# K chunks of a cached-attention decode kernel: in-place transposes in three parts instead of two

## The chip, the cores and the metric

The kernel runs on one core of a Trainium2 chip. Five engines of that core work from their own instruction queues: TensorE (PE, with its weight loads shown as PEld), VectorE (DVE), ScalarE (ACT), GpSimd (POOL) and SyncE (SP). SP does no arithmetic here; it issues nearly all the transfers from the chip's memory (HBM) into the core's working memory. The engines wait for each other through semaphores. The metric is the device time of one execution in microseconds (us), lower is better. A time is given as the median of several executions.

## The reference, cut to what matters

```python
def _A_ref(x, k_cache, v_cache, wq, wo):          # x [8,1,448]; caches [8, 8, 4096, 256]
    q = (x @ wq) -> [8, 16 heads, 1, 256]
    k = repeat(k_cache, 2, axis=1); v = repeat(v_cache, 2, axis=1)
    scores = einsum("bhqd,bhkd->bhqk", q, k) * 256 ** -0.5
    p = softmax(scores)
    o = einsum("bhqk,bhkd->bhqd", p, v)
    return o.reshape(8, 1, 4096) @ wo
x = A_x
x = x + _A_ref(layernorm(x), ...)                 # pass 0
x = x + _B_ref(layernorm(x), w1, w2, w3, w4)      # an MLP
x = x + _A_ref(layernorm(x), ...)                 # pass 1, the same caches again
x = x + _B_ref(layernorm(x), w1, w2, w3, w4)
```

Everything is bf16. There are 8 batch elements with one token each, 16 query heads and 8 key/value heads, 4096 cached positions and a head dimension of 256. K and V are 134 MB each, and both passes read the same two caches. The arithmetic per byte is small: each cached value is used for two query heads and then no more in that pass. (`_B_ref` also has a branch on shifted columns; with one token per sequence every shift brings in zeros alone, so the kernel computes only the MLP of `w3` and `w4`.)

## The kernel before

**Tiling.** The key/value heads are taken in four pairs, called `gp`. One task is one pass, one batch element and one `gp`. Its K, two heads of 4096 positions of 256 values, comes as four chunks of 1 MB; so does its V. A chunk lies in one of `NC = 15` slots of 8 KB in each of 128 partitions (line 72), as 16 positions of 256 values in each partition.

**What stays.** 11 of the chunks of a batch element are kept in their slots from pass 0 until pass 1 of that element (`kept`, line 63), and a twelfth is parked in PSUM (`away` and `back`, lines 723 and 730). While they are kept, only the few slots left over carry the stream of all other chunks. Slots in plenty and slots in short supply alternate, once for each batch element.

**The order of work.** It is written out by hand. `items` (line 538) is a list of chunks: K chunks of a task, interleaved one to one with the V chunks of the task before it. The loop at line 834 goes through it and emits for a K chunk: `transpose_k` (line 870), one piece of the small work that is spread between the chunks (`step`, line 871), then `scores` and, after every second chunk, the exponentials `exps`. For a V chunk it emits one piece of small work and then `pv`, 16 matmuls. After either, the chunk's slot goes back to the list `places`, `emit_loads` (line 945) issues the next transfer into a slot that is free in this order, and another piece of small work follows. Each engine executes its share in exactly that order. SP waits, for every transfer, until the last user of the slot is done: for a K slot this is the last matmul of `scores`, for a V slot the last matmul of `pv`.

**The small work.** The generators `first_half`, `chain`, `first_last`, `last` and `rest` (lines 456 to 504) hold the normalization of the softmax, the output projection, the MLP and the next query projection of a batch element. They are chains of short DVE, ACT and POOL instructions and groups of matmuls with 128x128 weights; each piece needs the one before.

**The K chunk.** The scores need the head dimension on the partitions. `transpose_k` transposes the chunk in place with DVE, in blocks of 32 by 32 words of 32 bits (two bf16 values each). A partition's row of a chunk is 16 positions (`y`) of 128 words; the 128 words are four quarters (`e`) of 32 words. The loop of line 689 takes two instructions, one for quarters 0 and 1 of all positions and one for quarters 2 and 3. `scores` (line 693) then runs eight rounds `n`, each with four matmuls (`k`) that write to four different groups of 32 PSUM partitions: rounds 0 to 3 read quarters 0 and 1, rounds 4 and 5 read quarter 2, rounds 6 and 7 read quarter 3. Some chunks are taken in twos (`also`), when they lie in neighbouring slots. In round 4, `between` may put the transpose of the previous task's probabilities ahead of the second half.

A matmul waits for the DVE instruction that wrote what it reads, so the first half's matmuls can run while the second half is transposed.

Of the kernel before, what the change touches and what calls it, by code (L numbers as in the profile page):

```python
# [10 lines left out]
U32 = mybir.dt.uint32  # L11
# [6 lines left out]
def kernel(  # L18
# [530 lines left out]
    def stays(it):  # L549
        n, kv, c = it  # L550
        return (tasks[n][2], kv, c) in kept

    def inside(it):
        n, kv, c = it
        return (tasks[n][2], kv, c) == inner
# [130 lines left out]
    def transpose_k(t):  # L686


        for half in range(2):
            w = t[:].bitcast(U32).rearrange("p (y e w) -> p y e w", e=2, w=64)[:, :, half]  # L690
            nc.vector.transpose(w, w)  # L691

    def scores(t, x, qbd, gp, also=None, between=None):
# [140 lines left out]
    for idx, it in enumerate(items):  # L834
# [12 lines left out]
        p = where[(b, gp), (kv, c)] if ps == 1 and (stays(it) or inside(it)) else where[it]  # L847
# [3 lines left out]
        if kv == 0:  # L851
# [17 lines left out]
            if not (ps == 1 and stays(it)):  # L869
                transpose_k(slot)  # L870
# [142 lines left out]
```

## Time and profile before

| | |
|---|---|
| median of 4 executions | 1114.28 us (1108.36 to 1118.52) |
| the profiled execution, whole | 1118.52 us |
| its span, first to last instruction | 1116.7 us |
| memory read in it | 446.77 MB |
| PE busy | 664.1 us (59%) |
| ACT busy / POOL busy | 124.5 us (11%) / 16.4 us (1%) |
| transfers of V, 1 MB each | 215, median 13.1 us from issue to landing |
| transfers of K, 1 MB each | 154, median 8.8 us from issue to landing |
| transfers of K, 2 MB each | 23, median 17.5 us |

A transfer's time from issue to landing includes its queueing behind the transfers issued before it, so a short one means few were ahead of it. The busy share of an engine is an average over stages with different limits; PE's is also modelled, since matmuls overlap. DVE's work is nearly all in one group: the 400 transposes of line 691, two for each of 200 K chunks. In the chain of work that ended last, the largest parts are waits for K and V transfers.

The last 13 us of the span have no cache transfer: they are the last output projection, the MLP of four batch elements and the store of the result, after the last V chunk has landed.

### The profile page before, as it was taken

The page shows a single profiled execution, that of the slowest core. Times are in us where ns is not written, and L with a number is a line of the kernel's source. Part 1 is how long each engine was busy: PE and PEld are TensorE (multiplying, and loading weights), DVE is VectorE, ACT ScalarE, POOL GpSimd, SP SyncE. Part 2 cuts the span into 40 slices and gives each one's busy share as a digit, 9 for nine tenths or more (in the row PEclk, how much of TensorE's full clock was granted, in tenths as well). Part 3 has the DMA queues.
Part 4 walks back from the last instruction along what each step waited for, and adds up shares of the span by engine and source line. Part 5 has one row for each costly group of instructions (what it writes and reads, how often), then busy time and mean ns, then how long its engine had stood idle before and what let it go on. Part 6 is the DMA issues. An engine that isn't in the chain of part 4 may idle for free. (4 is left out here: it accounts for less than half of the span.)

```text
span 1116.7 us, 33251 instructions
## 1 busy us (share of the span) xinstructions
PE 664.1 (59%) x15350; PEld 457.0 (41%) x15350; DVE 590.8 (53%) x1010; ACT 124.5 (11%) x362; POOL 16.4 (1%) x27
## 2 busy tenths in 40 slices
PE   3235567556754577536684466744676467847775
PEld 2123445334532354324452244523454345635554
DVE  4245554646355555546365563665637552665372
ACT  0001001100110011101011000200111001111010
POOL 0000000000000000000000000000000000000000
PEclk9999999655565557655555555765556555565565
DMA  9999999999999999999999999999999999999994
GB/s 347 386 426 419 418 382 416 419 411 394 418 423 421 391 407 421 424 419 388 397 417 421 421 384 413 416 423 417 391 421 420 410 389 402 420 417 364 404 419 188
DMA packets 62012, 448.92 MB, mean 402 GB/s; under 512 B 6569, under 2 KB 10545, under 8 KB 11313
## 3 DMA queue, kind: packets, MB, share of 16 engines
q1 hardware_dynamic: 61680, 446.42, 97.9%
q8 instruction: 120, 1.97, 0.7%
q10 hardware_dynamic: 192, 0.38, 0.2%
q14 instruction: 20, 0.16, 0.0%
HBM read 446.77 MB, written 0.01 MB: 400 GB/s over the span
## 5 line engine op out<-in xcount | busy, mean ns | idle before, releaser
L691 DVE STREAM_TRANSPOSE places<-places 128x1024 uint32<-128x1024 uint32 x400 | 468.4, 1218 | 282.5 <-DMA places<-in_A_k_cache_dram 277.4
L706 PE MATMUL sc<-places,qbd 128*8 128x128 bf16 (+1 forms) x6816 | 269.1, 311 | 252.9 <-DVE places L691 206.7
L761 PE MATMUL o<-places,ptw 128*8 128x256 bf16 x3968 | 244.3, 390 | 143.3 <-DMA places<-in_A_v_cache_dram 130.6
L706 PEld LDWEIGHTS <-qbd 128*8 128x8 bf16 x6816 | 165.4, 106 | 332.8 <-issue 160.7
L761 PEld LDWEIGHTS <-ptw 128*8 128x8 bf16 x3968 | 114.3, 111 | 190.2 <-issue 149.2
L715 ACT ACTIVATE p_n<-sc 128x256 bf16<-128x256 f32 x128 | 95.7, 748 | 835.2 <-PE sc L706 835.2
L316 DVE TENSOR_SCALAR qbd<-misc,quad 128x64 bf16<-128x64 f32 x64 | 13.8, 277 | 64.1 <-PE misc L310 64.1
L343 PEld LDWEIGHTS <-wo_sb 128*128 128x128 bf16 x1280 | 38.4, 102 | 20.9 <-issue 20.8
L290 PEld LDWEIGHTS <-wq_sb 128*128 128x128 bf16 x1152 | 35.8, 104 | 26.4 <-issue 18.0
L290 PE MATMUL misc<-xb,wq_sb 128*128 128x1 bf16 x1024 | 34.4, 165 | 4.7 <-ACT ptw L749 3.2
L343 PE MATMUL misc<-OT,wo_sb 128*128 128x1 bf16 x1024 | 34.8, 165 | 3.5 <-issue 3.5
L715 ACT ACTIVATION_READ_ACCUMULATOR p_n<-sc 128x1 f32 x128 | 33.8, 264 | 0.0
L749 ACT CAST ptw<-misc 128x128 bf16<-128x128 f32 x64 | 17.5, 274 | 123.5 <-PE misc L742 64.5
L447 PEld LDWEIGHTS misc<-R,o_sb 128*128 128x128 f32 x124 | 26.2, 293 | 9.7 <-issue 8.1
L240 POOL TENSOR_TENSOR t<-t,nhalf 128x2 f32<-128x2 f32 (+2 forms) x20 | 14.0, 704 | 1087.3 <-DVE t L254 1087.3
L447 PE MATMUL misc<-R,o_sb 128*128 128x8 f32 x124 | 28.9, 343 | 0.3 <-ACT o_sb L442 0.3
L416 PE MATMUL misc<-zm,one 128*128 128x8 f32 (+1 forms) x66 | 19.2, 364 | 13.0 <-DVE zm L408 11.3
L733 DVE STREAM_TRANSPOSE places<-store 128x512 uint32<-128x512 uint32 x32 | 20.1, 684 | 12.3 <-PE sc L706 12.3
L416 PEld LDWEIGHTS misc<-zm,one 128*128 128x128 f32 x66 | 16.3, 307 | 19.6 <-issue 12.4
L361 PEld LDWEIGHTS <-w_sb 128*128 128x128 bf16 x560 | 17.3, 105 | 10.5 <-issue 10.4
L361 PE MATMUL misc<-xb,w_sb 128*128 128x1 bf16 (+1 forms) x560 | 18.6, 166 | 4.4 <-DVE xb L267 2.2
L726 DVE STREAM_TRANSPOSE store<-places 128x512 uint32<-128x512 uint32 x32 | 20.0, 693 | 1.5 <-DMA places<-in_A_v_cache_dram 1.4
(93 smaller groups left out, 227.8 us busy)
## 6 DMA issues: line engine op xcount, KB each, us to landing
places<-in_A_v_cache_dram SPq DMA_DIRECT2D x215, 1024.0 KB, 13.1
places<-in_A_k_cache_dram SPq DMA_DIRECT2D x154, 1024.0 KB, 8.8
places<-in_A_k_cache_dram SPq DMA_DIRECT2D x23, 2048.0 KB, 17.5
wo_sb<-in_A_wo_dram SPq DMA_DIRECT2D x1, 3584.0 KB, 27.5
wq_sb<-in_A_wq_dram SPq DMA_DIRECT2D x3, 1024.0 KB, 10.2
w_sb<-in_B_w_dram SPq DMA_DIRECT2D x1, 1568.0 KB
w_sb<-in_B_w_dram SPq DMA_DIRECT2D x3, 448.0 KB, 19.0
places<-in_A_v_cache_dram SPq DMA_DIRECT2D x2, 512.0 KB, 19.2
```

What stands on the lines that cost most here:

```text
L290: nc.tensor.matmul(q_ps[:, j * Hq + h, :], w, xbs(nb)[:, xi, :], start=(fc == 0), stop=(fc == 3),)
L343: nc.tensor.matmul(y_ps[:, fc, :], w[:, i, at : at + 128], rhs(i), start=start, stop=stop, skip_group_check=open is not None,)
L361: nc.tensor.matmul(h_ps[:, c * nb : c * nb + nb], w, xbs(nb)[:, xi, :], start=(fc == 0), stop=(fc == 3),)
L416: nc.tensor.matmul(z_ps, ones, zm[:], start=True, stop=True)
L447: nc.tensor.matmul(ot_ps[:, j], o_sb[:].rearrange("p (i j) -> p j i", j=2)[:, j], R[:], start=True, stop=True)
L691: nc.vector.transpose(w, w)
L706: nc.tensor.matmul(sc[32 * k : 32 * k + 8, 128 * x : 128 * (x + nx)], qbd[:, ep, gp].rearrange("p a h -> p (a h)"), v, start=(n == 0), sto ...
L715: nc.scalar.activation(p_sb[:, :, :, 2 * u : 2 * u + 2].rearrange("p t i x -> p x t i"), sc[:, 256 * u : 256 * u + 256].rearrange("p (x t ...
L726: nc.vector.transpose(store[n][:].bitcast(U32), slot[:].bitcast(U32)[:, 512 * n : 512 * n + 512])
L733: nc.vector.transpose(slot[:].bitcast(U32)[:, 512 * n : 512 * n + 512], store[n][:].bitcast(U32))
L749: nc.scalar.copy(ptw[:, :, :, 6:8], pt_ps.rearrange("p t k (a h) -> p a (t k) h", a=4),)
L761: nc.tensor.matmul(o_ps[32 * q : 32 * q + 8, 0:256], ptz[:, at : at + 8], v[:, y * Dh : (y + 1) * Dh], start=(begin and y < 4), stop=(y >= ...
```

## The change

`transpose_k` issues three instructions for each chunk instead of two: quarters 0 and 1 in one, then quarter 2, then quarter 3. The first is the same as before (16 runs of 64 words in each partition); the other two have 16 runs of 32 words.

```diff
     def transpose_k(t):
 
 
-        for half in range(2):
-            w = t[:].bitcast(U32).rearrange("p (y e w) -> p y e w", e=2, w=64)[:, :, half]
+        for e0, e1 in ((0, 2), (2, 3), (3, 4)):
+            w = t[:].bitcast(U32).rearrange("p (y e w) -> p y e w", e=4, w=32)[:, :, e0:e1]
             nc.vector.transpose(w, w)
```

`scores` has no change in its text. In the built program PE, ACT, POOL and SP have the same instructions in the same order as before. DVE has one more transpose for each K chunk. On PE one more matmul of each chunk waits for DVE: round 4 now waits for quarter 2 alone, and round 6 for quarter 3.

## The prediction

> **What bounds the kernel now.** I read the page first, for the engines and the transfers.
>
> ```profile
> span 1116.7 us, 33251 instructions
> DMA  9999999999999999999999999999999999999994
> GB/s 347 386 426 419 418 382 416 419 411 394 418 423 421 391 407 421 424 419 388 397 417 421 421 384 413 416 423 417 391 421 420 410 389 402 420 417 364 404 419 188
> q1 hardware_dynamic: 61680, 446.42, 97.9%
> ```
>
> The transfer queue that SP fills is busy 97.9% of the span, in every slice but the last. No engine comes near: DVE has 590.8 us, 53%. The kernel is bound by reading the caches. But the GB/s row shows more than the 9s: it runs at 416 to 426 and dips to between 364 and 397 at regular intervals, one dip for each batch element. A busy queue can still be a thin one. So the second view is the table of stages, with borders laid around two of the dips.
>
> ```profile
> core 0: us, PE busy (x) PEld busy (x) DVE busy (x) ACT busy (x) POOL busy (x), PEclk, DMA share, GB/s
> 570.00:640.00 70.00, 39.03 (x870) 25.53 (x866) 42.50 (x44) 7.89 (x22) 0.00 (x0) 0.55 1.01 422
> 640.00:700.00 60.00, 40.63 (x918) 28.39 (x912) 29.68 (x72) 6.48 (x22) 1.25 (x2) 0.50 0.99 399
> 820.00:890.00 70.00, 40.19 (x961) 27.00 (x960) 40.68 (x56) 9.63 (x28) 0.00 (x0) 0.60 1.01 421
> 890.00:950.00 60.00, 41.71 (x980) 29.83 (x984) 26.94 (x61) 6.48 (x19) 1.25 (x2) 0.50 0.98 392
> ```
>
> The reader is to see that DVE is busier in the stages that run at full rate (42.50 of 70 us) than in those that dip (29.68 of 60). DVE's load as such costs nothing. Full rate is about 421. All eight dips (130 to 180, 240 to 300, 370 to 430, 500 to 570, 640 to 700, 770 to 820, 890 to 950, 1000 to 1060 us, at 393, 403, 400, 397, 399, 401, 392 and 385) lose, against 421, 60 x (1 - 399/421) = 3.1 us in the fourth of those I show and so on: 3.3 + 2.6 + 3.0 + 4.0 + 3.1 + 2.4 + 4.1 + 5.1 = about 28 us together. That is all that a faster or slower handling of slots can act on from inside the stream; the start (first 50 us) and the 13 us after the last transfer have no K transposes on their path to speak of.
>
> The third view is the timeline inside a dip, which shows why it dips (lines in between left out).
>
> ```profile
> 649.36 0.33 SPq L678 DMA_DIRECT2D places<-in_A_k_cache_dram  x1
> ...
> 654.30 0.16 DVE L216 TENSOR_REDUCE t<-t 128x2 f32<-128x8 f32 x1
> ...
> 654.51 0.50 PEld L221 LDWEIGHTS misc<-t,one 128*128 128x128 f32 x2 [0.53 <-DVE t L216]
> ...
> 655.03 1.03 PE L761 MATMUL o<-places,ptw 128*8 128x256 bf16 x16
> ...
> 656.10 0.33 SPq L678 DMA_DIRECT2D places<-in_A_v_cache_dram  x1
> 656.70 2.37 DVE L691 STREAM_TRANSPOSE places<-places 128x1024 uint32<-128x1024 uint32 x2 [0.83 <-DMA places<-in_A_k_cache_dram]
> ...
> 658.00 0.60 PE L706 MATMUL sc<-places,qbd 128*8 128x128 bf16 x16 [1.94 <-DVE places L691]
> ...
> 659.13 0.60 PE L706 MATMUL sc<-places,qbd 128*8 128x128 bf16 x16 [0.53 <-DVE places L691]
> ...
> 659.77 0.33 SPq L678 DMA_DIRECT2D places<-in_A_k_cache_dram  x1
> ```
>
> This is one round of one K slot. Its transfer is issued at 649.36, has landed at 656.70 when DVE starts at once, the second half's matmuls end at 659.73, and SP issues into the slot at 659.77. Round: 10.41 us, of which 7.34 in flight and 3.07 on the core. A V slot works alike: the matmuls of L761 end at 656.06, SP issues at 656.10. Two K and two V slots carry the stream here, 4 MB a round; at 421 GB/s that is 9.96 us. So the round is 0.45 us longer than the transfers alone need, and each tenth taken off the core's 3.07 us can come back, until 0.45 is used up.
>
> **The change, part by part.**
>
> *DVE's extra instruction.* The nearest rows for a transpose of 512 words in a partition:
>
> ```profile
> L691 DVE STREAM_TRANSPOSE places<-places 128x1024 uint32<-128x1024 uint32 x400 | 468.4, 1218 | 282.5 <-DMA places<-in_A_k_cache_dram 277.4
> L726 DVE STREAM_TRANSPOSE store<-places 128x512 uint32<-128x512 uint32 x32 | 20.0, 693 | 1.5 <-DMA places<-in_A_v_cache_dram 1.4
> ```
>
> ```profile
> 94.22 2.50 DVE L726 STREAM_TRANSPOSE store<-places 128x512 uint32<-128x512 uint32 x4
> ...
> 186.62 9.12 DVE L691 STREAM_TRANSPOSE places<-places 128x1024 uint32<-128x1024 uint32 x8
> ```
>
> By whole durations, two of 512 cost 2 x 693 - 1218 = 168 ns more than one of 1024. But the merged rows show that transposes in a row overlap: four of 512 take 2.50 us, so a pitch of (2.50 - 0.69)/3 = 0.60; eight of 1024 take 9.12, a pitch of (9.12 - 1.20)/7 = 1.13. By pitch the cost is 2 x 0.60 - 1.13 = 0.07 us. The Trainium skill (VectorE: DVE Perf Modes, "The DRAIN you can't avoid") speaks against the change here: the next operation does not start until the pipe is empty, and one is told to minimize the number of operations. By that rule 168 ns a chunk, 200 x 0.168 = 34 us of DVE; by the trace 200 x 0.07 = 14 us. I take the trace, and keep 0.17 as the upper end. Lower end zero: L726 writes PSUM, and a write to the same memory may be no dearer. Shorter runs (32 words instead of 64) number 16 in either shape; 1024 in 16 runs has the pitch of 1.13 and 512 in one run 0.60, both the words at one per about 1.04 ns with 0.06 over, so the breaks between runs cost nothing that I can see.
>
> Where does this lie? In the full stages beside a stream that does not wait for it: the cover is 27.5 of 70 us idle on DVE. In the dips it lies in the path of every chunk.
>
> *The release of a K slot.* Before: transposes 2.37, then 0.06 to the first matmul of the second half, then 0.60. After: first part unchanged, 1.17 to its successor's start, then 0.60, then the last part 0.69: 2.46, so +0.09. Behind it come 8 matmuls instead of 16. One takes 0.31 (mean of the L706 row), four run side by side, so the 16 are four groups: (0.60 - 0.31)/3 = 0.10 a group, and two groups fewer save 0.19. Quarter 2's eight are done by then (ready at 1.17 + 0.69 = 1.86, done about 2.3). Net -0.10 us in a K release. Ends: -0.19 if a quarter costs no overhead, about 0 if parts do not overlap. PE's additional wait per chunk blocks what stands behind it (the small work, then L761), which PE reaches 0.10 earlier for the same reason; PE idles 0.53 us between the halves now, so it had nothing else there.
>
> *The release of a V slot.* The pieces of small work on DVE stand behind the transposes and go +0.07 later (ends 0 and +0.17). Where PE needs them before L761, as L221 at 654.51 waits for L216, the V slot comes free 0.07 later. Where it does not, 0.10 earlier. The rows of SP's waits name both kinds of release about equally often in this stage, so I count V as even.
>
> *The sum.* The stage from 640 to 700 has 16 transposes, 8 chunks: four rounds of two K slots. Four rounds x 0.10 = 0.4 us, eight dips: 3.2 us at most by this share. V rounds stand still, and a part of every dip is a late start rather than a tight round, so I take somewhat over half: -2 us. Against the profiled execution's own 1118.52 (span 1116.7 and 1.8 around it): 1116.5. This execution was the slowest of the four shown, 4.2 above the median of 1114.28, so the forecast is 1112.
>
> Whether there is anything to recover rests on the rate that the stream could have. The Trainium skill (DMA: Bandwidth & Descriptors, "Where 436 GB/s comes from") says that for transfers from HBM the memory's limit of about 358 GB/s for a core binds. By that rule the dips, at 385 and more, would be above the limit and nothing could be won or lost by slots. The trace has 70 us at 422; the measurement decides, and the dips are a shortage of slots.
>
> **The rivals.**
>
> *Nothing moves* (0.27). The stream is bound by bytes, and what the K slots gain the V slots lose. For: the queue's 97.9%, and 28 us as the whole of what slots can act on. Time: 1114.
>
> *Slower through the V slots* (0.18). Mechanism: in the dips a DVE piece behind the transposes holds PE ahead of L761, and V's release decides when the queue refills. For: the pair of rows at 654.30 and 654.51, where PE idles 0.53 for exactly that. Against: it holds for a part of the pieces only. Price: 64 chunks in the eight dips x 0.07 = 4.5 us, so 1119; with the rule's 0.17 it is 11 us, 1125. It decides as soon as the V releases, not the K releases, end the thin moments, and a quarter's pitch is above 0.60.
>
> *Much more comes back* (0.05). If both kinds of slot gain 0.10 to 0.19 in every chunk and the next dip starts with a fuller queue: 64 x 0.19 = 12 us, 1102. The limit is 28. Against: 0.19 needs quarters without overhead.
>
> That the parts are not waited for singly is a rival only where PE lags behind DVE; the 0.53 us of idle says it doesn't in the dips.
>
> **How the numbers follow.** Forecast, a gain of 0 to 6 us: 0.50. Two executions of the same kernel differ by up to 10 us here, so a median has some 3 us of its own. The range takes the forecast, the rival of no change and most of the slower one: 1104 to 1121. About 1% (11 us) is what a measurement can tell from no change: faster by that 0.04, slower by that 0.09, within 0.87.
>
> **What would show each step.** Two thirds of the L691 instructions at 128x512 with a mean near 0.69, DVE busy up by about 200 x 0.17 = 34 us (busy counts whole durations) while the pitch is 0.60. In a dip: the landing of a K chunk to SP's next issue 2.97 instead of 3.07, the last group of L706 x8 with 0.40. Dip stages at 400 to 403 instead of 399, full stages unchanged at 421. I am wrong if a quarter takes over 0.75, if the dips fall below 395, or if the full stages change.

## The result, and the profile after

The changed kernel takes 1106.31 us in the median of 32 executions (1102.53 to 1114.11), against 1111.54 us for the kernel before in 53 executions (1104.27 to 1118.52). The ratio is 0.9958, with a 95% interval of 0.9943 to 0.9972: 4.7 us less, between 3.1 and 6.3. Beside one of the experiments it was measured again: 0.9943 (0.9916 to 0.9970). The profiled execution took 1108.63 us.

From the page of the changed kernel, the lines that answer to those of before:

```profile
span 1106.7 us, 33460 instructions
...
PE 685.1 (62%) x15350; PEld 459.1 (41%) x15350; DVE 603.0 (54%) x1210; ACT 124.5 (11%) x362; POOL 16.4 (1%) x27
...
GB/s 340 383 424 422 420 402 418 421 409 402 418 423 420 400 415 422 420 420 401 420 422 422 420 394 410 412 423 412 405 402 415 420 394 415 420 419 397 414 419 191
...
q1 hardware_dynamic: 61680, 446.42, 98.4%
```

The dips in the GB/s row are still there, but the deepest is 394 where it was 364. The queue is a little better filled, 98.4% for 97.9%. DVE works 12.2 us more, as it must with 200 more instructions. The same four stages as before (busy time by engine, granted clock, share and GB/s):

```profile
570.00:640.00 70.00, 37.10 (x763) 23.74 (x763) 41.16 (x64) 7.63 (x22) 0.00 (x0) 0.51 1.01 418
640.00:700.00 60.00, 44.02 (x968) 30.19 (x969) 29.12 (x74) 6.70 (x20) 1.25 (x2) 0.50 1.00 405
820.00:890.00 70.00, 44.23 (x1010) 29.67 (x1014) 44.22 (x76) 10.38 (x30) 0.00 (x0) 0.57 1.01 415
890.00:950.00 60.00, 44.06 (x1051) 30.39 (x1044) 30.40 (x70) 6.79 (x20) 1.25 (x2) 0.50 1.00 406
```

The two dips rise from 399 to 405 and from 392 to 406. The stages at full rate do not rise; where one reads a little lower (415 for 421) the borders, laid for the kernel before, now cut into the next dip, since the stream runs ahead: from 630 to 640 us the rate is 398, where it was 423. Counted by bytes instead of by time, so that the borders play no part, the stretch from the 50th to the 440th MB took 27.8 us longer than at 421 GB/s before and 17.7 us longer after. The profiled execution of before was the longest of its kernel's and the medians differ by 5.2 us, about half of these 10. All of the gain lies in the dips.

The two groups of transposes in the changed kernel, from the table that keeps shapes apart:

```profile
L691 DVE STREAM_TRANSPOSE places<-places 128x512 uint32<-128x512 uint32 x400 | 252.4, 669 | 0.0
L691 DVE STREAM_TRANSPOSE places<-places 128x1024 uint32<-128x1024 uint32 x200 | 246.6, 1233 | 268.9 <-DMA places<-in_A_k_cache_dram 262.4 <-issue 4.4 <-PE o L761 1.8
```

And one K chunk with the V chunk behind it, in the same place of the program in both kernels (the chunk whose transposes are followed by the cast of line 451), from the timelines. Before:

```profile
646.29 2.37 DVE L691 STREAM_TRANSPOSE places<-places 128x1024 uint32<-128x1024 uint32 x2 [0.86 <-DMA places<-in_A_k_cache_dram]
...
648.72 0.60 PE L706 MATMUL sc<-places,qbd 128*8 128x128 bf16 x16 [0.53 <-DVE OT L451]
...
649.36 0.33 SPq L678 DMA_DIRECT2D places<-in_A_k_cache_dram  x1
...
650.19 1.03 PE L761 MATMUL o<-places,ptw 128*8 128x256 bf16 x16
...
651.26 0.33 SPq L678 DMA_DIRECT2D places<-in_A_v_cache_dram  x1
```

After:

```profile
640.57 2.43 DVE L691 STREAM_TRANSPOSE places<-places 128x1024 uint32<-128x1024 uint32 x3 [1.51 <-DMA places<-in_A_k_cache_dram]
641.87 0.98 PE L706 MATMUL sc<-places,qbd 128*8 128x128 bf16 x24 [1.34 <-DVE places L691]
...
643.05 0.39 PE L706 MATMUL sc<-places,qbd 128*8 128x128 bf16 x8 [0.21 <-DVE OT L451]
...
643.48 0.33 SPq L678 DMA_DIRECT2D places<-in_A_k_cache_dram  x1
...
644.31 1.03 PE L761 MATMUL o<-places,ptw 128*8 128x256 bf16 x16
...
645.38 0.33 SPq L678 DMA_DIRECT2D places<-in_A_v_cache_dram  x1
```

Read both from the start of the transposes, which is also the landing. The transposes take 2.43 us instead of 2.37. But 24 of the 32 matmuls are through by then, and the last 8 take 0.39 instead of the 0.60 of the last 16. SP issues the next K at 2.91 us instead of 3.07. And the next V follows at 4.81 instead of 4.97: all that PE has between the two kinds of matmul moves up as one. Over the K chunks that start in the eight dips, the last matmul on K ends 2.87 us after the transposes' start in the median, where it was 3.02; the last matmul on the V chunk behind it is 0.14 to 0.16 us earlier in 52 of 64 cases, and later in 9.

Seven of those nine, each later by 0.06 or 0.07, are the case that the prediction feared, where DVE's small work stands between: the matmuls of L221 wait for L216. It comes once in every dip but the first (timeline of the changed kernel):

```profile
645.55 2.43 DVE L691 STREAM_TRANSPOSE places<-places 128x1024 uint32<-128x1024 uint32 x3 [2.49 <-DMA places<-in_A_k_cache_dram]
...
648.87 0.59 PE L221 MATMUL misc<-t,one 128*128 128x2 f32 x2 [0.46 <-DVE t L216]
649.39 1.03 PE L761 MATMUL o<-places,ptw 128*8 128x256 bf16 x16
...
650.46 0.33 SPq L678 DMA_DIRECT2D places<-in_A_v_cache_dram  x1
```

Here SP issues the V transfer 4.91 us after the start of the transposes; before it was 656.10 - 651.26 = 4.84.

### The profile page after: what moved, and what is told of

The parts are those of the page before. It is cut to its first block, busy times and chain, and to the rows that moved or that the text cites. A ratio compares the mean times of both kernels' runs of the same rounds, so it can differ in the third digit from the quotient of the medians.

```text
span 1106.7 us, 33460 instructions
## 1 busy us (share of the span) xinstructions
PE 685.1 (62%) x15350; PEld 459.1 (41%) x15350; DVE 603.0 (54%) x1210; ACT 124.5 (11%) x362; POOL 16.4 (1%) x27
## 3 DMA queue, kind: packets, MB, share of 16 engines
q1 hardware_dynamic: 61680, 446.42, 98.4%
HBM read 446.77 MB, written 0.01 MB: 404 GB/s over the span
## 5 line engine op out<-in xcount | busy, mean ns | idle before, releaser
L691 DVE STREAM_TRANSPOSE places<-places 128x512 uint32<-128x512 uint32 (+1 forms) x600 | 480.2, 857 | 268.9 <-DMA places<-in_A_k_cache_dram 262.4
L706 PE MATMUL sc<-places,qbd 128*8 128x128 bf16 (+1 forms) x6816 | 286.7, 311 | 230.6 <-DVE places L691 194.2
L761 PE MATMUL o<-places,ptw 128*8 128x256 bf16 x3968 | 248.6, 396 | 135.7 <-DMA places<-in_A_v_cache_dram 125.7
L343 PEld LDWEIGHTS <-wo_sb 128*128 128x128 bf16 x1280 | 38.8, 103 | 21.1 <-issue 21.0
L343 PE MATMUL misc<-OT,wo_sb 128*128 128x1 bf16 x1024 | 35.0, 165 | 2.3 <-issue 2.3
L361 PE MATMUL misc<-xb,w_sb 128*128 128x1 bf16 (+1 forms) x560 | 18.6, 166 | 4.2 <-DVE xb L267 2.2
```

Of the source, the lines that this page charges most:

```text
L343: nc.tensor.matmul(y_ps[:, fc, :], w[:, i, at : at + 128], rhs(i), start=start, stop=stop, skip_group_check=open is not None,)
L361: nc.tensor.matmul(h_ps[:, c * nb : c * nb + nb], w, xbs(nb)[:, xi, :], start=(fc == 0), stop=(fc == 3),)
L706: nc.tensor.matmul(sc[32 * k : 32 * k + 8, 128 * x : 128 * (x + nx)], qbd[:, ep, gp].rearrange("p a h -> p (a h)"), v, start=(n == 0), sto ...
L761: nc.tensor.matmul(o_ps[32 * q : 32 * q + 8, 0:256], ptz[:, at : at + 8], v[:, y * Dh : (y + 1) * Dh], start=(begin and y < 4), stop=(y >= ...
```

## The experiments

Two theories of where the gain came from stood against each other first. *Release*: only the time from a chunk's landing to the end of its last matmul counts, because that is when slots come free in the dips. *Parts*: more and smaller parts are better as such. Later the first was divided: does the K slot decide, the V slot, or both?

The table collects what was measured; the second and third columns are read off each timeline at the same chunk as above (from the start of the transposes to SP's next issue of K and of V). It is one chunk only; where the other chunks of the dips differ, the text says so, from the same 64 chunks in each trace. Ratios are to the kernel before on the same chip.

| kernel | K issue at, us | V issue at, us | ratio (95% interval) |
|---|---|---|---|
| before | 3.07 | 4.97 | 1 |
| the change | 2.91 | 4.81 | 0.9958 (0.9943 to 0.9972) |
| the change, measured again | | | 0.9943 (0.9916 to 0.9970) |
| quarter 3 ahead of quarter 2 | 3.12 | 5.02 | 1.0014 (0.9990 to 1.0037) |
| one part | 3.43 | 5.33 | 1.0142 (1.0109 to 1.0176) |
| three quarters, then one | 2.90 | 4.80 | 0.9977 (0.9952 to 1.0001) |
| four quarters | 2.97 | 4.87 | 0.9961 (0.9931 to 0.9991) |
| before, V matmuls ahead of small work | 3.06 | 4.54 | 1.0009 (0.9982 to 1.0035) |
| the change, V matmuls ahead of small work | 2.91 | 4.39 | 0.9960 (0.9933 to 0.9987) |
| the change, V later (16 matmuls) | 2.91 | 5.21 | 1.0056 (1.0029 to 1.0082) |
| the change, V later (8 matmuls) | 2.92 | 5.01 | 0.9993 (0.9966 to 1.0019) |
| before, V later (8 matmuls) | 3.07 | 5.17 | 1.0087 (1.0064 to 1.0110) |

**1. Three parts without the earlier release.**

```diff
-        for e0, e1 in ((0, 2), (2, 3), (3, 4)):
+        for e0, e1 in ((0, 2), (3, 4), (2, 3)):
```

> Three parts as in the change, but quarter 3 is transposed before quarter 2, so that round 4 of the scores waits for the last part and 16 matmuls follow it, as in the kernel before. Theory 'release' (the time is set by how long after its landing a chunk's last matmul ends, in the eight dips of some four rounds each): landing to the last matmul's end 3.02 + 0.06 = 3.08 us, V slots 0.06 later too, 32 rounds x 0.06 = +2 us against before. Rival 'parts' (more, smaller parts help as such, or the gain is of the measurement): -5 us as in the change. Rival 'DVE load costs' : +2 us or more, but then the whole transpose in one instruction has to be faster than before.

Measured: 1113.27 us against 1110.59, ratio 1.0014. The timeline shows the intended state:

```profile
643.69 2.43 DVE L691 STREAM_TRANSPOSE places<-places 128x1024 uint32<-128x1024 uint32 x3 [1.23 <-DMA places<-in_A_k_cache_dram]
644.99 0.60 PE L706 MATMUL sc<-places,qbd 128*8 128x128 bf16 x16 [1.07 <-DVE places L691]
...
646.17 0.60 PE L706 MATMUL sc<-places,qbd 128*8 128x128 bf16 x16 [0.59 <-DVE OT L451]
...
646.81 0.33 SPq L678 DMA_DIRECT2D places<-in_A_k_cache_dram  x1
```

The same three DVE instructions, 2.43 us, but 16 matmuls wait for the last. The whole gain is gone. So it did not come from parts as such, and the price of the extra instruction, with the release 0.06 us later that it brings, is 1.6 us, with an interval from -1.1 to 4.1: not told from zero.

**2. One part.**

```diff
-        for e0, e1 in ((0, 2), (2, 3), (3, 4)):
+        for e0, e1 in ((0, 4),):
```

> The chunk is transposed by one instruction of 2048 words; all 32 matmuls follow it. DVE work falls by about 0.06 us a chunk. Theory 'release': the instruction takes about 2.27 us, then eight groups of four matmuls take about 1.08 with the first wait: 3.35 us after landing instead of 3.02, V slots as much later: 32 rounds x 0.33 = +10 us, some more if the queue runs dry more often. Rival 'DVE load costs': faster than before by about 2 us.

Measured: 1127.37 against 1110.59, ratio 1.0142, about 16 us. DVE has less to do than in any other version (L691 is busy 456.4 us, before 468.4), and the kernel is the slowest of this family.

```profile
650.20 2.30 DVE L691 STREAM_TRANSPOSE places<-places 128x2048 uint32<-128x2048 uint32 x1
...
652.56 1.02 PE L706 MATMUL sc<-places,qbd 128*8 128x128 bf16 x32 [0.81 <-DVE OT L451]
653.63 0.33 SPq L678 DMA_DIRECT2D places<-in_A_k_cache_dram  x1
```

All 32 matmuls, 1.02 us, follow the transpose; K is issued at 3.43. "DVE load costs" is out. The direction and the mechanism were expected, the size was short: 16 us, not 10. The chunk shown is not the worst kind: 15 of the 64 chunks release K 0.69 us or more later than before, and in 14 of them PE also has the transpose of the probabilities (L742) to do before K's last matmuls. The mean over the 64 is 0.44.

**3. Three quarters, then one.**

```diff
-        for e0, e1 in ((0, 2), (2, 3), (3, 4)):
+        for e0, e1 in ((0, 3), (3, 4)):
```

> Two parts of three quarters and one quarter: as many DVE instructions as before, but only 8 matmuls behind the last. Theory 'release': 1.70 us to the start of the second part, 0.67 for it, 0.44 for the last 8 matmuls: 2.81 us after landing (2.87 in the change, 3.02 before), unless the 24 matmuls of the first part are not done in time (they need about 0.7 us, the second part 0.67). 32 rounds x 0.21 = -6.5 us against before, 1 to 2 us better than the change. Theory 'parts': no better than before, as the number of parts is the same.

Measured: 1109.22 against 1110.59, ratio 0.9977. Better than before by the middle of its interval (whose end just reaches no change), but not better than the change as expected. The timeline shows a chunk that explains it:

```profile
654.51 2.37 DVE L691 STREAM_TRANSPOSE places<-places 128x1536 uint32<-128x1536 uint32 x2 [1.97 <-DMA places<-in_A_k_cache_dram]
...
656.34 0.60 PE L706 MATMUL sc<-places,qbd 128*8 128x128 bf16 x16 [1.55 <-DVE places L691]
...
657.09 0.60 PE L706 MATMUL sc<-places,qbd 128*8 128x128 bf16 x16
...
657.74 0.33 SPq L678 DMA_DIRECT2D places<-in_A_k_cache_dram  x1
```

PE begins only 1.83 us after the landing and then has all 32 matmuls before it; in this chunk the transpose of the probabilities stands between them as well. The issue comes at 3.23 us, where the changed kernel is at 2.91 (656.36 to 659.27 in its timeline). PE itself has become the last link. Such chunks are 16 of the 64 (14 with the transpose of the probabilities between); there the last matmul on K ends 0 to 0.17 us later than before. In the other 48 it ends 0.16 or 0.17 us earlier, as in the change. A part must be small at the end, and the first one early enough for PE to be done with it.

**4. Four quarters.**

```diff
-        for e0, e1 in ((0, 2), (2, 3), (3, 4)):
+        for e0, e1 in ((0, 1), (1, 2), (2, 3), (3, 4)):
```

> Four parts of one quarter each. The matmuls behind the last part are 8 as in the change, but DVE has one more instruction. Theory 'release': landing to the last matmul's end 2.87 + 0.06 = 2.93 us, 32 rounds x 0.09 = -3 us against before, 2 us behind the change. Theory 'parts': better than the change, -8 us or so against before.

Measured: 1107.84 against 1110.59, ratio 0.9961. K is issued at 2.97, as worked out. The time is that of the change within its interval, so this run does not tell 3 us from 5; the 8 us "or so" of "parts" lies only just outside the interval, whose end (0.9931) is 7.7 us.

**5 and 6. V earlier, with two parts and with three.** In the loop over the chunks, the piece of small work that stood ahead of the V matmuls is emitted behind them:

```diff
-            step(idx)
             if final and gp in free:
+                step(idx)
                 pv_cols(oc, slot, c, gp)
...
                 begun.add((ps, b, g8))
+                step(idx)
```

> The kernel before, two parts, with one move in the hand-written order: for a V chunk the 16 matmuls on V are emitted ahead of the piece of small work, not behind it. K slots are released as before, V slots about 0.9 us earlier wherever the piece has matmuls (median end of the V matmuls 4.8 us after the K chunk's landing now). Theory 'release, K and V alike': the change shortened both kinds by 0.15 us for 4.7 us, so V alone by 0.9 gives about 0.9 / 0.15 x 2.35 = 14 us, as far as the dips have it to give (28 us in the profile of before). Theory 'K slots decide': the K round stays as it is, within 2 us of before.

> The same move with the three parts of the change. If the dips are nearly gone through the V slots, the three parts add little, under 2 us beyond the move alone; if K slots decide, the change's full 5 us on top of the move.

Measured: 1110.51 against 1110.01 with two parts (1.0009), and 1106.53 with three (0.9960). In the first:

```profile
645.40 2.37 DVE L691 STREAM_TRANSPOSE places<-places 128x1024 uint32<-128x1024 uint32 x2 [1.23 <-DMA places<-in_A_k_cache_dram]
...
648.46 0.33 SPq L678 DMA_DIRECT2D places<-in_A_k_cache_dram  x1
648.87 1.03 PE L761 MATMUL o<-places,ptw 128*8 128x256 bf16 x16
...
649.94 0.33 SPq L678 DMA_DIRECT2D places<-in_A_v_cache_dram  x1
```

V is issued at 4.54 instead of 4.97, more than twice what the change gave it (0.43, not the 0.9 expected: 16 of the 32 matmuls of L343 still stand ahead of it). Over the 64 chunks V's last matmul is 0.38 us earlier in the median, though in 22 it hardly moves. No gain shows: the interval goes from 2.0 us faster to 3.9 slower. The three parts on top bring their full gain. The move is not clean: DVE's pieces wait longer for PE (its waits at line 331 for the matmuls of L343 go from 18.6 to 28.8 us in all), so the run says that V alone does not do it, not that V is worth nothing.

**7 and 8. One slot more.** Ten chunks are kept instead of eleven, with two parts and with three:

```diff
-    kept = [(GP - 1, kv, n) for n in range(4) for kv in range(2)] + [(GP - 2, 0, n) for n in range(3)]
+    kept = [(GP - 1, kv, n) for n in range(4) for kv in range(2)] + [(GP - 2, 0, n) for n in range(2)]
```

> The kernel before with 10 chunks kept between the passes instead of 11, so one slot more for the stream; 8 chunks of 1 MB are read again: 8 x 1.05 MB / 421 GB/s = 20 us more, less what the dips give back. With five slots in the stream the dips should be nearly gone: 1111 + 20 - 20 to 25, so 1106 to 1111.

> The same with the three parts of the change. Theory 'release' (a slot's release matters only where slots are short): within 1.5 us of the run with two parts and 10 kept. Rival 'parts help as such, slots or no slots': 5 us faster than that run.

Measured: 1151.50 and 1151.32 us against 1110.01. The level was expected wrongly by 40 us. From the page and from SP's waits of the run with two parts, one of them for 95 to 125 us:

```profile
GB/s 336 385 425 378 381 421 420 403 349 420 419 424 362 421 420 423 423 365 421 419 422 422 366 418 419 421 419 375 419 419 422 362 419 419 423 297 418 419 420 189
```

```profile
SPq L678 <- PE sc L706: 19.3, 1, 19.3
```

The page shows that the extra bytes came out as expected (455.15 MB read, for 446.77: 20 us at 421 GB/s). The other half of the 41.5 us does not come from them. The long shallow dips are gone; in their place stands one short, deep one for each batch element, and in most of them SP waits 19.3 us in one go for one slot. (How the planner's choice of slots makes that wait was not followed.) In the stretches that were dips, the rate is 421 now (140 to 220 us), and there the three parts change nothing: 1151.50 against 1151.32. That fits a gain that comes from earlier releases in the dips alone, and it was the expected difference, though at an unexpected level.

**9 to 12. V held back.** Small matmuls into unused columns of a PSUM bank go ahead of the matmuls on V; nothing of the output depends on them:

```diff
         g = 2 * gp + a // 2
+        for _ in range(16):    # 8 in the last two runs
+            nc.tensor.matmul(misc[0:8, 492:500], ptz[:, 0:8], identb[:, 0:8], start=True, stop=True)
         for y in range(16):
```

> The three parts of the change, with 16 small matmuls (8 columns by 8, into unused columns of a PSUM bank; they add nothing to the output) ahead of the 16 matmuls on every V chunk, so that V slots come free some 0.3 to 0.5 us later while K slots stay at 2.87 us after landing. Theory 'K slots decide': at most 2 us above the change, still faster than before. Theory 'K and V alike': 0.4 us of V delay eats more than the whole gain, +1 to +3 us against before.

> The changed kernel itself on the chip of the run beside it, as its comparison: 0.994 to 0.997 of before.

Measured: 1119.38 with V held back and 1105.84 for the change itself beside it, against 1112.28 before. "K slots decide", which runs 5 and 6 had suggested, falls: K is issued at 2.91, as in the change, and the kernel is slower than before. So the amount was halved, and tried on both kernels:

> The three parts of the change with 8 of the small matmuls ahead of the V matmuls (16 moved the V release by 0.33 us, so 8 by about 0.16): K slots 0.15 us earlier than before, V slots where they were before (with 0.1 to 0.2 us more on PE for the small work behind them). Theory 'the later of the two binds' (SP issues K, V, K, V strictly in turn, so that a gain needs both): within 2 us of before. Theory 'K slots decide': -4 to -5 us. Theory 'K and V alike': -2 us.

> The kernel before with the same 8 small matmuls: K slots as before, V slots 0.16 us later. 'The later of the two binds': +5 us (0.16 at the price of 31 us for each us that the change showed). 'K slots decide': 0 to +1 us. 'K and V alike': +2 to +3 us.

Measured: 1110.60 against 1110.76 (0.9993) and 1119.72 (1.0087). In the first, K is 0.15 us earlier than before, and in the chunk of the table V is nearly where it was:

```profile
648.28 2.43 DVE L691 STREAM_TRANSPOSE places<-places 128x1024 uint32<-128x1024 uint32 x3 [0.97 <-DMA places<-in_A_k_cache_dram]
...
651.20 0.33 SPq L678 DMA_DIRECT2D places<-in_A_k_cache_dram  x1
...
653.29 0.33 SPq L678 DMA_DIRECT2D places<-in_A_v_cache_dram  x1
```

That is 2.92 and 5.01, and the time is that of before. But this chunk hides what the small matmuls do elsewhere. The chunk ahead of it, in the kernel before and in run 11:

```profile
641.45 2.36 DVE L691 STREAM_TRANSPOSE places<-places 128x1024 uint32<-128x1024 uint32 x2
...
645.99 0.33 SPq L678 DMA_DIRECT2D places<-in_A_v_cache_dram  x1
```

```profile
643.48 2.42 DVE L691 STREAM_TRANSPOSE places<-places 128x1024 uint32<-128x1024 uint32 x3
...
647.16 0.29 PE L759 MATMUL misc<-identb,ptw 128*8 128x8 bf16 x6 [0.30 <-DVE rz L419]
...
648.43 0.33 SPq L678 DMA_DIRECT2D places<-in_A_v_cache_dram  x1
```

Here V is issued at 4.95 us instead of 4.54. The small matmuls (L759) write to the bank `misc`, which DVE's small work reads; so they wait for DVE themselves (0.30 us for L419 here, up to 3.1 us for L451 elsewhere), and DVE's pieces wait for them (L299 for 32.8 us in all). Over the 64 chunks V's last matmul in run 11 is within 0.04 us of before in half, but 0.18 us or more later in 27; the mean is 0.16 later. Run 11 is therefore not K alone: K comes 0.15 earlier, V on average as much later, and together they leave the time as it was.

Run 12, at the chunk of the table:

```profile
644.64 2.37 DVE L691 STREAM_TRANSPOSE places<-places 128x1024 uint32<-128x1024 uint32 x2 [0.67 <-DMA places<-in_A_k_cache_dram]
...
647.71 0.33 SPq L678 DMA_DIRECT2D places<-in_A_k_cache_dram  x1
...
649.81 0.33 SPq L678 DMA_DIRECT2D places<-in_A_v_cache_dram  x1
```

K stays at 3.07, V goes from 4.97 to 5.17 (0.22 us later in the mean of the 64), and the kernel loses 9.7 us. That is twice what was expected, and more than the 6.2 us of run 9, with V later still and K earlier. Between runs 11 and 12, which have the same small matmuls, the three parts are worth about 9 us. Because the small matmuls also make PE and DVE wait for each other, and put off the small work behind them, these runs price more than V's release.

What is shown: the gain hangs on how little is left for PE behind the last part, not on the number of parts (runs 1, 2 and 4). V released earlier with K unchanged brings no gain that can be seen (run 5). And a later V, held back in this way, does harm (runs 9 and 12). What K alone would bring, with V where it was, is left open: no run holds V still. A price for each kind is open too. That SP's issuing in strict turn, K, V, K, V, is what ties the two together is argued, not shown: no run issues them from two queues.

## Why the prediction was right in its direction and short in its size

- *Bound by transfers, with a reserve only in the dips.* Right: the gain lies in the dips, the full stages stay at about 421, and with one slot more the change does nothing. The reserve of 0.45 us a round was read off a single round, though. The round before it, from SP's issue of K at 644.50 to that at 654.32, took 9.82 us, less than the 9.96 that the transfers alone were said to need. (The dip from 640 to 700 us, with its loss of 3.1 us, is the fifth of the eight, not the fourth.)
- *DVE's extra instruction costs its pitch, not its duration.* Right. DVE's busy time rose by 603.0 - 590.8 = 12.2 us, 0.06 a chunk; the prediction had 0.07 from the trace and 0.17 by the rule of the Trainium skill (VectorE: DVE Perf Modes, "The DRAIN you can't avoid") that the next operation waits for an empty pipe. The prediction left out the exception in the same paragraph, "A next op that is not held starts earlier". The transposes here do start earlier: a quarter takes 669 ns, and the next transpose starts 593 ns after it began. Its sign to look for was wrong in one point: it expected busy time to count whole durations and rise by 34 us. Overlapping instructions are counted once.
- *The release of a K slot, -0.10.* Right in kind, mis-sized: 3.07 to 2.91, about -0.15. The last part is 0.67 long and not 0.69, so that the transposes end 0.06 later and not 0.09; and 8 matmuls take 0.21 less than 16, where two groups at 0.10 gave 0.19.
- *The release of a V slot: "so I count V as even".* This is the step that failed. It rested on SP's waits for K and for V being about equally many, which does not say how many V chunks have a DVE piece ahead of them. In the dips V comes 0.15 us earlier in 52 of 64, exactly as K does, and the feared wait occurs in 7. The pair of lines at 654.30 and 654.51, which the prediction showed, comes about once in a dip.
- *The sum, -2.* Four rounds, eight dips and 0.15 instead of 0.10 are 4.8 us; measured 4.7. But that sum counts K alone, and V moved too; how much of the gain K would have brought with V standing still, as the prediction had it, no run shows. The close agreement may be luck. So is, in part, the place of the result within the forecast of 0 to 6 us, a range so wide that the mistake about V could not show in it. The prediction's "somewhat over half" was a discount for late starts that the result does not show.
- *The rivals.* "Slower through the V slots" named a real mechanism: run 12 loses 9.7 us with V about 0.2 later. At that rate the feared 0.07 in every chunk would cost some 3 us, an estimate; the prediction had 4.5, since it counted 64 chunks there and 32 rounds (of two K slots each) in its own sum. It did not come about because the delay occurs in few chunks. "Nothing moves" supposed that V's loss cancels K's gain. Run 11 shows that outcome, with V later on average by as much as K is earlier.

## What to carry to other kernels

Where a stream of transfers is short of buffers, look at the last link between landing and release: cut the work there so that little is left behind the last piece, even if the engine ahead of it does more instructions, but begin early enough that the engine behind it is not swamped. Follow the release of every kind of buffer that the issuing queue fills, and count how often a feared wait occurs before giving it half the weight. A saturated queue's busy share hides this; the bytes per second by stage show it.

## What was not expected of the hardware

Transposes of 512 words take 669 ns from SBUF to SBUF, a little less than the 693 to PSUM from which they were estimated, and one of 2048 words takes 2.30 us where two of 1024 take 2.37: about 0.06 us for each further instruction from one to four parts (2.30, 2.37, 2.43, and 2.49 for four quarters in that run's timeline).
